# A two-layer kernel on one core: the second layer's output matmuls of a slice issued together instead of in two halves

## The chip, the core and the metric

The kernel runs on one core of a Trainium2 chip. Five engines work side by side, each through its own queue in order: PE (matrix multiply), DVE (vector), ACT (scalar functions), POOL (general) and SP, which here issues the DMAs. The metric is device time in microseconds; less is better. A kernel's time is the median of several runs, and one more execution is taken with the hardware profiler, from which all rows below are read.

## The reference

8192 tokens of width 192 pass through a dynamic convolution of 7 taps (softmax over the taps, 8 heads), then through two layers with an inner width of 2048:

```
x = attn_out.reshape(B * S, D)                       # 8192 x 192
h = x @ w_in                                         # 192 x 2048
P = a[0] + a[1] * h + a[2] * h2 + a[3] * h3
Q = 1.0 + np.abs(b[0]) * np.abs(h) + np.abs(b[1]) * h2
x = (P / (Q + 1e-06)) @ w_out                        # first layer
h = x @ w_in2
return (h * np.clip(h + 3.0, 0.0, 6.0) / 6.0) @ w_out2   # second layer
```

## The kernel before

The tokens are split into 32 blocks of 256, and a block's inner width into 4 slices of 4 chunks of 128, so there are 128 slices `sl`, numbered through; block `b` has slices 4b to 4b+3. Weights are decoded from 64-bit words at the start and stay on the chip.

**First layer, per slice.** PE multiplies the block's input with the slice's weights (`in1`, two halves of two chunks, ten matmuls each, split into high and low parts in fp32r) into the PSUM tile `h1` (two buffers). ACT makes `u` (absolute value), `w` and `l`; POOL multiplies `w` by `u` (`pool_q`, line 293); ACT takes the logarithm (`act_ln`, 308), the exponential (`act_exp`, 313) and one more step on `w` (`act_q`, 317); DVE does `dve_t`, `dve_t2` and `dve_hi` (322), which writes `ghi`, the high part of the activation. POOL's `pool_m` (330) then multiplies `w` by `ghi` into `m`, DVE's `dve_d` (335) subtracts and sets `h1` free, and POOL's `pool_lo` (343) writes `glo`, the low part. PE's `out1` (361 to 366, two halves of ten matmuls) takes `ghi` and `glo` and sums into `y1` over the block's four slices. After the block's last slice `mid_y`, `mid_head` (ACT), `mid_f` (PE, the fold at line 231), `mid_tail` (ACT) and `lo1h`, `lo1t` (DVE) bring `y1` into the form of an input.

**Second layer, per slice, some five slices later.** PE's `in2` (two halves of ten matmuls, into two PSUM buffers `h2`, which it shares with the transposes and the fold), ACT's `act_r2` (387, per half, writes `r`), DVE's `dve_g2` (393, per half, writes half of `g2`; two buffers), and PE's `out2` (409): for each of four chunks and two groups of 128 tokens a matmul in fp32, which the trace records as two passes, summed into `y2`. After a block's last slice ACT's `evac` copies `y2` out and SP stores it.

**Beside it** the convolution for later blocks: `conv_mul` (162, DVE, in the first blocks also POOL), `conv_sum` (176, DVE), the softmax steps, `x_dup`, `x_hi` and the transpose `xT`.

**What sets the order.** Nothing is written in program order. `op`/`add` record each step with an engine, an estimated cost, a priority (a due time, lines 650 to 700), the steps it comes after and the buffers it takes. `plan()` then simulates all engines with these estimates, always placing the step that can start earliest, ties by priority, and the kernel emits the steps in that order. The queue of every engine is fixed by that list; on the chip each engine waits at the head of its queue for what its next instruction needs. A change to one step's cost, due time or conditions can so move steps on all engines. Numbers of slices below are found in the trace by counting: every step's line appears once per slice (or half).

## Time and profile before

| | |
|---|---|
| runs | 1442.16, 1443.62, 1447.23 us |
| median | 1443.62 us |
| profiled execution, span from first to last instruction | 1440.4 us |
| the median of the runs above that span | 3.2 us |
| PE busy / DVE / ACT / POOL | 1314.3 / 1221.8 / 1044.6 / 1007.2 us |

The profile gives no time of its own for the profiled execution beyond its span. Busy time is the sum of an engine's instructions; a matmul's end is modelled and matmuls overlap, so PE's busy time says where it has work, while the spacing of starts says how long that takes. The first 150 us are loading and decoding of weights, with PE mostly idle; then the pipeline runs until the last block is drained.

### The profile page before, as it was taken

To read this page: it belongs to the slowest core of one execution; us is meant where nothing else is said; L and a number is where in the kernel's file an instruction comes from. 1 tells how busy PE (TensorE), PEld (TensorE's weight loads), DVE (VectorE), ACT (ScalarE), POOL (GpSimd) and SP (SyncE) were. 2 spreads that over 40 slices of the span, in tenths; PEclk is the share of its full clock that TensorE was granted. 3 is DMA by queue.
4 is the path that set the end of the run, shared out by engine and by line. 5 is a ranking of instruction groups with operands and counts; after the bars stand their busy time and mean duration, and the time that the engine had idled before them with its cause. 6 is when DMAs were issued, how large, how long until landed. Compare 5 with 4: busy or idle time off the path is not lost.

```text
span 1440.4 us, 23889 instructions
## 1 busy us (share of the span) xinstructions
PE 1314.3 (91%) x9920; PEld 1297.6 (90%) x9920; DVE 1221.8 (85%) x1197; ACT 1044.6 (73%) x1290; POOL 1007.2 (70%) x433
## 2 busy tenths in 40 slices
PE   1333899999999999999999999999999999999998
PEld 1233899999999999999999999999999999999998
DVE  5999988999988888889888888898888888988662
ACT  2654678787778777777787777777777777777772
POOL 4766677767676777677777776777777777777760
PEclk9666999999999999999999999999999999999999
DMA  7444001000010101001010100001010000000000
GB/s 184 120 137 121 28 7 37 7 27 11 7 37 7 37 7 37 6 1 37 7 38 6 37 6 10 28 6 37 7 37 6 32 12 1 7 7 7 6 7 12
DMA packets 18070, 42.17 MB, mean 29 GB/s; under 512 B 2088, under 2 KB 12328, under 8 KB 17960
## 3 DMA queue, kind: packets, MB, share of 16 engines
q1 hardware_dynamic: 17960, 40.63, 9.2%
q8 instruction: 78, 1.28, 0.4%
q14 instruction: 32, 0.26, 0.1%
HBM read 30.14 MB, written 6.29 MB: 25 GB/s over the span
## 4 chain that ended last, share of the span: by engine, by line
DVE 30%; POOL 23%; PE 19%; ACT 13%; issue 12%; DMA 2%; POOLq 0%; SPq 0%; DVEq 0%; ACTq 0%
POOL m L330 15%; PE h L252 9%; POOL w L293 8%; DVE ghi L322 7%; PE y L409 5%; DVE h L301 4%; DVE g L393 4%; DVE m L335 4%; ACT r L313 3%; DVE l L297 3%; ACT r L387 2%; DVE xc L176 2%; ACT l L286 2%; ACT w L317 2%; ACT u L274 2%
## 5 line engine op out<-in xcount | busy, mean ns | idle before, releaser
L330 POOL TENSOR_TENSOR m<-w,ghi 128x1024 f32<-128x1024 f32 x128 | 350.6, 2739 | 317.7 <-DVE ghi L322 248.1
L252 PE MATMUL h<-xh,wtail 128*128 128x256 f32 x2048 | 417.3, 286 | 1.1 <-DVE xh L212 1.1
L409 PE MATMUL y<-wo,g 128*128 128x192 f32 x2048 | 374.8, 325 | 0.0
L409 PEld LDWEIGHTS y<-wo,g 128*128 128x128 f32 x2048 | 329.5, 190 | 0.1
L293 POOL TENSOR_TENSOR w<-w,u 128x1024 f32<-128x1024 f32 x128 | 307.3, 2400 | 27.5 <-ACT w L279 27.5
L252 PEld LDWEIGHTS h<-xh,wtail 128*128 128x128 f32 x2048 | 323.7, 194 | 1.6 <-DVE xh L212 1.6
L343 POOL TENSOR_TENSOR glo<-m,r 128x1024 fp32r<-128x1024 f32 x128 | 309.8, 2420 | 13.8 <-DVE m L335 10.5
L308 ACT ACTIVATE r<-w,ceps 128x1024 f32<-128x1024 f32 x128 | 147.3, 1151 | 220.4 <-POOL w L293 220.4
L335 DVE SCALAR_TENSOR_TENSOR m<-h,acol,m 128x1024 f32<-128x1024 f32 x128 | 164.0, 1281 | 132.2 <-POOL m L330 132.2
L387 ACT ACTIVATE r<-h,half 128x512 f32<-128x512 f32 x256 | 173.6, 678 | 63.1 <-PE h L252 63.1
L252 PE MATMUL h<-xh,win0hi 128*128 128x256 f32 x512 | 164.7, 322 | 52.7 <-DVE m L335 52.0
L393 DVE SCALAR_TENSOR_TENSOR g<-r,h 128x512 f32<-128x512 f32 x256 | 174.0, 682 | 22.9 <-ACT r L387 22.9
L322 DVE SCALAR_TENSOR_TENSOR ghi<-h,acol,r 128x1024 fp32r<-128x1024 f32 x128 | 163.9, 1280 | 16.3 <-ACT r L313 16.1
L176 DVE TENSOR_REDUCE xc<-prod 128x192 f32<-128x1344 f32 x64 | 166.9, 2607 | 0.0
L297 DVE TENSOR_TENSOR l<-h,l 128x1024 f32<-128x1024 f32 x128 | 155.8, 1217 | 11.6 <-ACT l L286 10.0
L301 DVE SCALAR_TENSOR_TENSOR h<-l,acol,h 128x1024 f32<-128x1024 f32 x128 | 164.2, 1283 | 0.5
L252 PE MATMUL h<-xh,win1hi 128*128 128x256 f32 x512 | 162.0, 316 | 1.6 <-DVE xh L212 0.9
L361 PE MATMUL y<-ghi,wo1h 128*128 128x256 f32 x512 | 157.7, 308 | 2.1 <-DVE xl L205 2.1
L279 ACT ACTIVATE w<-u,bab 128x1024 f32<-128x1024 f32 x128 | 159.2, 1244 | 0.0
L252 PEld LDWEIGHTS h<-xh,win0hi 128*128 128x128 f32 x512 | 100.7, 197 | 60.9 <-issue 32.0
L286 ACT ACTIVATE l<-h,acol 128x1024 f32<-128x1024 f32 x128 | 154.1, 1204 | 1.9 <-DVE h L301 1.9
L252 PE MATMUL h<-xl,win0hi 128*128 128x256 f32 x512 | 147.9, 289 | 0.0
(73 smaller groups left out, 2962.9 us busy)
## 6 DMA issues: line engine op xcount, KB each, us to landing
x<-in_x_dram SPq DMA_DIRECT2D x14, 960.0 KB
st<-in_moe_w_out_dram SPq DMA_DIRECT2D x16, 384.0 KB
out_dram<-osb SPq DMA_DIRECT2D x32, 192.0 KB
st<-in_moe_w_in_dram SPq DMA_DIRECT2D x8, 512.0 KB
wtail<-th SPq DMA_DIRECT2D x16, 256.0 KB
st<-in_moe_w_in_dram SPq DMA_DIRECT2D x8, 256.0 KB
x<-in_x_dram SPq DMA_DIRECT2D x4, 472.5 KB
wg<-in_weight_gen_dram SPq DMA_DIRECT2D x16, 112.0 KB
```

What stands on the lines that cost most here:

```text
L176: nc.vector.tensor_reduce(out=xc[b][:, s, 0:D], in_=prod.pop((b, s)).rearrange("p k h g -> p (h g) k"), axis=AX.X, op=ALU.add,)
L252: nc.tensor.matmul(out=dst, lhsT=l[:, fs], rhs=r, start=(n == 0), stop=(n == len(seq) - 1), skip_group_check=True,)
L293: nc.gpsimd.tensor_tensor(out=e["w"], in0=e["w"], in1=e["u"], op=ALU.mult)
L297: nc.vector.tensor_tensor(out=e["l"], in0=h, in1=e["l"], op=ALU.mult)
L301: nc.vector.scalar_tensor_tensor(out=h, in0=e["l"], scalar=acol[:, 1:2], in1=h, op0=ALU.add, op1=ALU.mult)
L322: nc.vector.scalar_tensor_tensor(out=fl(ghi), in0=h, scalar=acol[:, 0:1], in1=e["r"], op0=ALU.add, op1=ALU.mult)
L330: nc.gpsimd.tensor_tensor(out=m, in0=e["w"], in1=fl(g1[sl][0]).bitcast(F32), op=ALU.mult)
L335: nc.vector.scalar_tensor_tensor(out=e["m"], in0=h, scalar=acol[:, 0:1], in1=e["m"], op0=ALU.add, op1=ALU.subtract)
L343: nc.gpsimd.tensor_tensor(out=fl(glo), in0=e["m"], in1=e["r"], op=ALU.mult)
L387: nc.scalar.activation(out=r, in_=h, func=AF.Relu, scale=1.0 / 6.0, bias=half[:, 0:1])
L393: nc.vector.scalar_tensor_tensor(out=g2[sl][:, hh * 2 : hh * 2 + 2, :].rearrange("p f t -> p (f t)"), in0=r, scalar=1.0, in1=h, op0=ALU.mi ...
L409: nc.tensor.matmul(out=y2[b][:, s, :], lhsT=g[:, f, s * P : (s + 1) * P], rhs=wo2[:, n, :], start=(n == 0 and s == 0), stop=(n == NF - 1), ...
```

## The change

The step `out2` is one per slice instead of one per half. It issues all four chunks (16 passes), is planned with a cost of 2.6 instead of 1.3, has one due time (`t + 7 * T + 6.4`, where the halves had `5.4` and `6.4`), comes after the second half of `dve_g2`, and what waited for the second half (`evac`, the release of `g2`) waits for the whole.

```
-    def out2(sl, half):
+    def out2(sl):
         b, q = divmod(sl, NG)
-        fs = range(half * GF // 2, (half + 1) * GF // 2)
-        if q == 0 and 0 in fs:
+        if q == 0:
             y2[b] = ps_y.tile([P, SUB, D], F32, tag="y2", name="y2")
-        g = g2[sl]
-        for f in fs:
+        g = g2.pop(sl)
+        for f in range(GF):
             n = q * GF + f
             for s in range(SUB):
                 nc.tensor.matmul(
                     out=y2[b][:, s, :], lhsT=g[:, f, s * P : (s + 1) * P], rhs=wo2[:, n, :],
                     start=(n == 0 and s == 0), stop=(n == NF - 1), skip_group_check=True,
                 )
-        if GF - 1 in fs:
-            g2.pop(sl)
...
-        add("evac", "ACT", 0.45, t + 10 * T + 8.2, evac, b, after=[("out2", b * NG + NG - 1, 1)])
+        add("evac", "ACT", 0.45, t + 10 * T + 8.2, evac, b, after=[("out2", b * NG + NG - 1)])
...
-                take=[("g2", 2, [("out2", sl, 1)])] if k == 0 else [])
-            add("out2", "PE", 1.3, t + 7 * T + 5.4 + k, out2, sl, k,
-                after=[("dve_g2", sl, k), done["o2", 2 * q + k]] + prev("out2", k),
-                take=[("y2", 1, [("evac", b)])] if q + k == 0 else [])
+                take=[("g2", 2, [("out2", sl)])] if k == 0 else [])
+        add("out2", "PE", 2.6, t + 7 * T + 6.4, out2, sl,
+            after=[("dve_g2", sl, 1), done["o2", 2 * q], done["o2", 2 * q + 1], ("out2", sl - 1)],
+            take=[("y2", 1, [("evac", b)])] if q == 0 else [])
```

`plan()` gives another order for PE, ACT, DVE and POOL from about slice 4 on; from about slice 32 to slice 121 it repeats every eight slices. Three places in that repeat, at slices 66 to 68:

POOL before, from `pool_lo` of slice 66 on (`w` is `pool_q`, `m` is `pool_m`, `glo` is `pool_lo`; numbers tell buffers apart):

```order
L343 TENSOR_TENSOR glo_7503<-m_7450,r0_7398 128x1024
L330 TENSOR_TENSOR m_7556<-w_7466,ghi_7541 128x1024
L293 TENSOR_TENSOR w_7579<-w_7579,u_7568 128x1024
L343 TENSOR_TENSOR glo_7610<-m_7556,r0_7509 128x1024
L330 TENSOR_TENSOR m_7667<-w_7579,ghi_7653 128x1024
```

POOL now, the same place:

```order
L343 TENSOR_TENSOR glo_7496<-m_7450,r0_7398 128x1024
L330 TENSOR_TENSOR m_7552<-w_7466,ghi_7527 128x1024
L343 TENSOR_TENSOR glo_7592<-m_7552,r0_7498 128x1024
L293 TENSOR_TENSOR w_7581<-w_7581,u_7564 128x1024
L330 TENSOR_TENSOR m_7677<-w_7581,ghi_7662 128x1024
```

`glo` of slice 67 now stands ahead of `w` of slice 68. This is so in one slice of eight; in the other seven the order is the old one.

ACT before, from `act_l` of slice 67 on (`r2` is `act_r2`; `r0` is the logarithm at line 308 and the exponential at 313):

```order
L286 ACTIVATE l_7480<-h1_7402,acol_81 128x1024
L387 ACTIVATE r2_7489<-h2_7452,half_85 128x512
L308 ACTIVATE r0_7509<-w_7466,ceps_84 128x1024
L387 ACTIVATE r2_7514<-h2_7491,half_85 128x512
L313 ACTIVATE r0_7509<-r0_7509 128x1024
L317 ACTIVATE w_7466<-w_7466 128x1024
```

ACT now:

```order
L286 ACTIVATE l_7480<-h1_7401,acol_81 128x1024
L387 ACTIVATE r2_7493<-h2_7452,half_85 128x512
L308 ACTIVATE r0_7498<-w_7466,ceps_84 128x1024
L313 ACTIVATE r0_7498<-r0_7498 128x1024
L317 ACTIVATE w_7466<-w_7466 128x1024
L387 ACTIVATE r2_7539<-h2_7502,half_85 128x512
```

The second `r2` left its place between logarithm and exponential. In slices 67 and 71 it stands behind the exponential's successor, in 68, 69 and 70 ahead of the logarithm, and in 64, 65 and 66 it is where it was.

PE before, from the end of the first half of `in1` of slice 68 on:

```order
L252 MATMUL h1_7516<-xh_7463,win0lo_87 128x256
L252 MATMUL h1_7516<-xh_7463,wtail0_90 128x256 x2
L252 MATMUL h2_7529<-xh_7273,win1hi_88 128x256
L252 MATMUL h2_7529<-xl_7275,win1hi_88 128x256
L252 MATMUL h2_7529<-xh_7273,win1lo_89 128x256
```

PE now:

```order
L252 MATMUL h1_7515<-xh_7463,win0lo_87 128x256
L252 MATMUL h1_7515<-xh_7463,wtail0_90 128x256 x2
L361 MATMUL y1_7324<-ghi_7434,wo1h_92 128x256
L362 MATMUL y1_7324<-ghi_7434,wo1l_93 128x256
L363 MATMUL y1_7324<-ghi_7434,wo1s_94 128x256
L365 MATMUL y1_7324<-glo_7496,wo1h_92 128x256
```

`out1` of slice 66 now follows the first half of `in1` of slice 68; before, the first half of `in2` of slice 62 and the second half of `in1` stood ahead of it.

## Rows read from the trace of the kernel before

**Rows 1.** Busy time by stage: us, then engines' busy us (instructions), PEclk, DMA, GB/s.

```profile
190.00:305.00 115.00, 114.98 (x890) 114.48 (x890) 104.06 (x95) 92.25 (x110) 83.25 (x35) 1.00 0.05 16
...
300.00:1300.00 1000.00, 982.38 (x7513) 971.16 (x7512) 871.72 (x848) 766.99 (x935) 730.49 (x292) 1.00 0.05 18
```

**Rows 2.** The page: span, and the chain that ended last, by engine.

```profile
span 1440.4 us, 23889 instructions
...
DVE 30%; POOL 23%; PE 19%; ACT 13%; issue 12%; DMA 2%; POOLq 0%; SPq 0%; DVEq 0%; ACTq 0%
```

**Rows 3.** Waits from 300 to 1300 us: who waited for whom, total us, times, longest.

```profile
POOL m L330 <- DVE ghi L322: 182.9, 73, 3.4
...
PE yf L231 <- DVE g L393: 10.3, 25, 0.4
...
PE h L252 <- DVE m L335: 6.4, 22, 0.4
```

**Rows 4.** Timeline of PE: start, us, instruction, shapes, count, [idle before <-releaser].

```profile
721.53 0.67 PE L231 MATMUL yf<-ys,fold 128*128 128x256 f32 x2 [0.43 <-DVE g L393]
...
803.98 0.67 PE L231 MATMUL yf<-ys,fold 128*128 128x256 f32 x2 [0.42 <-DVE g L393]
...
806.87 1.47 PE L409 MATMUL y<-wo,g 128*128 128x192 f32 x8
808.04 0.41 PE L361 MATMUL y<-ghi,wo1h 128*128 128x256 f32 x1
808.29 0.28 PE L362 MATMUL y<-ghi,wo1l 128*128 128x256 f32 x1
808.41 0.28 PE L363 MATMUL y<-ghi,wo1s 128*128 128x256 f32 x1
```

**Rows 5.** Chain of waits in the span's last stretch: start, us, what.

```profile
1420.83 1.30 PE y L409 x8
```

**Rows 6.** Chain of waits from 718 to 801 us.

```profile
767.95 2.40 POOL m L330
...
773.79 0.67 ACT r L387
...
776.89 3.53 POOL m L330
```

**Rows 7.** Timeline of POOL at slices 66 to 68.

```profile
782.72 2.41 POOL L343 TENSOR_TENSOR glo<-m,r 128x1024 fp32r<-128x1024 f32 x1
786.96 2.39 POOL L330 TENSOR_TENSOR m<-w,ghi 128x1024 f32<-128x1024 f32 x1 [1.82 <-DVE ghi L322]
790.21 2.39 POOL L293 TENSOR_TENSOR w<-w,u 128x1024 f32<-128x1024 f32 x1 [0.86 <-ACT w L279]
```

**Rows 8.** Timeline of ACT at slice 68.

```profile
788.89 1.24 ACT L279 ACTIVATE w<-u,bab 128x1024 f32<-128x1024 f32 x1
...
792.63 1.15 ACT L308 ACTIVATE r<-w,ceps 128x1024 f32<-128x1024 f32 x1 [2.30 <-POOL w L293]
793.69 0.67 ACT L387 ACTIVATE r<-h,half 128x512 f32<-128x512 f32 x1
794.26 1.04 ACT L313 ACTIVATE r<-r 128x1024 f32<-128x1024 f32 x1
```

**Rows 9.** Timeline of DVE at slices 66 to 68.

```profile
776.64 1.55 DVE L162 TENSOR_TENSOR prod<-x,wk 128x1344 f32<-128x1344 f32 x1
...
789.80 1.28 DVE L335 SCALAR_TENSOR_TENSOR m<-h,acol,m 128x1024 f32<-128x1024 f32 x1
...
793.45 2.93 DVE L162 TENSOR_TENSOR prod<-x,wk 128x1344 f32<-128x1344 f32 x1
796.30 0.68 DVE L393 SCALAR_TENSOR_TENSOR g<-r,h 128x512 f32<-128x512 f32 x1
796.90 1.27 DVE L322 SCALAR_TENSOR_TENSOR ghi<-h,acol,r 128x1024 fp32r<-128x1024 f32 x1
```

**Rows 10.** Timeline of PE: the first half of `in1` of slice 68.

```profile
782.42 0.41 PE L252 MATMUL h<-xh,win0hi 128*128 128x256 f32 x1
```

## The prediction

> **What bounds the kernel now.** The start is no use here: up to about 150 us weights are loaded and decoded, and the first output matmul of the second layer comes after that, so nothing before it can change. I read the stages behind it. From 190 to 305 us TensorE is busy for 114.98 of 115 us; from 300 to 1300 us it is busy for 982.38 of 1000 us, at a granted clock of 1.00 in both [rows 1]. So TensorE is close to being the bound, but in the long stage it is not quite it. The span's own chain says the same: the work that ended last runs for 30% through DVE and 23% through POOL and only 19% through PE [rows 2].
>
> The list of waits for the long stage shows how little of PE's time there has a releaser: 10.3 us where the fold matmul waits for the second layer's activation on DVE, 6.4 us where the first layer's input matmuls wait for DVE, while POOL sits 182.9 us waiting for DVE's `ghi` [rows 3]. The order repeats every eight slices (two blocks of tokens are four slices each). Between two fold matmuls eight slices apart lie 803.98 - 721.53 = 82.45 us [rows 4]. The PE work in it: 480 matmuls at 0.12 us (start to start, 808.29 to 808.41, [rows 4]), 128 passes of the second layer's output at 0.162 (1.30 us for eight, [rows 5]) and about 2 us of transposes and folds (an estimate from the fold's 0.67 us for two, overlapped), 57.6 + 20.7 + 2 = 80.3 us. So PE stands still for 82.45 - 80.3 = 2.1 us in eight slices, and no more than that can be won by taking waits away.
>
> What holds the 82.45 us is a ring through the other engines, seen in the chain of waits inside these eight slices [rows 6]: POOL `m` (2.40 us, 3.53 where DVE's convolution multiply began just ahead of it), POOL `w` of the next slice (2.39, [rows 7]), ACT's logarithm (1.15), an ACT step `r` of the second layer (0.67) that has nothing to do with it but stands between, ACT's exponential (1.04, [rows 8]), DVE `ghi` (1.27, [rows 9]), and POOL `m` again. It has hardly any slack. This is what I cost the change against: not against PE's work, which stays the same, but against the queue positions that shift on ACT, DVE and POOL, because the planner lays out all engines anew.
>
> **The joined matmuls themselves.** Count and size stay: 128 slices of 16 passes. Two things could differ. First, a switch between these fp32 matmuls and the fp32r ones around them might cost a restart, of which the change would save one for nearly every slice. The rows say it doesn't: eight passes start at 806.87, the next kind at 808.04, its second matmul at 808.29. From 806.87 to 808.29 is 1.42 us, and eight times 0.162 plus one 0.12 is 1.416 [rows 4, 5]. The long 0.41 us row right behind is a matmul recorded early, not time lost. A switch costs at most 0.005 us, 0.6 us in all; I take 0. Second, a new wait: all four chunks need both halves of the activation. But in the built order the wait for the second half stands at the first matmul of the second half, not at the head of the eight, so the first 1.30 us run as before. At each of the eight places of the repeat I set the new PE position against the time at which the second activation half ends; the nearest is output 61, whose second half is due at 790 or later (its PE position is the old one), while its activation is the DVE step just ahead of the `m` that (2) below puts at 789.25. Taken at 0; if one place in eight missed by 0.5 us this would be 0.5 per repeat.
>
> **What the new order moves, per eight slices.** (1) On ACT the step `r` stands between logarithm and exponential in every slice of the repeat before; after, in five of eight it doesn't: it is behind the exponential or ahead of the logarithm. Its place costs 794.26 - 793.69 = 0.57 us on the ring [rows 8], so up to 2.85 us could leave the ring.
>
> (2) On POOL, in one slice of eight (67, 75, ...), `glo` now stands ahead of the next slice's `w`. Before, `w` started at 790.21, as soon as ACT's own `w` (788.89 plus 1.24) was there [rows 7, 8]. After, `w` waits for `glo` and that for DVE's `m`. Worked through: the exponential 0.57 earlier puts `m` on POOL at 786.96 - 0.57 = 786.4, to 788.8 (2.39 us). DVE's `m` started at 789.80, behind one activation half that is still ahead of it, so it can come only about as much earlier, 789.25, and ends 1.28 later at 790.5. `glo` (2.41) runs to 792.95, `w` (2.39) to 795.35, the logarithm (1.15) to 796.5, the exponential (1.04) to 797.5. `ghi` of slice 68 stood at 796.90 before [rows 7 to 9]. So `w`, 2.75 us later, makes `ghi` only 0.6 us later: before, `ghi` stood behind a convolution multiply that was held up to 2.93 us (1.55 where nothing holds it) and an activation half, until 796.90 [rows 9].
>
> (3) On PE, output matmuls 66 of the first layer now come two places ahead, right behind the input matmuls of slice 68, at 782.42 + 1.2 = 783.6; their fourth matmul needs `glo` of 66, which POOL ends at 782.72 + 2.41 = 785.13 [rows 7, 10]. A new wait of 785.13 - 784.0 = 1.1 us on PE. Queued behind it are the second half of input 68, second-layer input 62 (which itself moves behind three more runs of ten matmuls, 3.6 us) and all that follows. PE has this 1.1 us to give, since of its 2.1 us some go away: one of the two waits at the fold matmul (0.43 us in its row, [rows 4]) vanishes because the fold moves behind 1.2 us more of matmuls, and one of those at the input matmuls too, since DVE's `m` behind the earlier exponential at 71 comes earlier [rows 3].
>
> (4) The 0.6 us of (2) goes on through `m`, DVE's `m`, the reduction and `ghi` of 69, all tight. At slice 70 the ring wins about 0.25 us back, not 0.57, since the `r` step ahead of the logarithm waits for a PE half that (3) made late. At 71 the exponential is 0.57 earlier, but DVE then takes the activation half behind ACT's next step and the reduction starts late by what is left. Net I get +0.3 us for eight slices, against 82.45. The bounds from the same rows: if (2)'s 0.6 is swallowed and one `r` step is won, -0.57; if (3)'s whole 1.1 us reaches the ring, +1.1.
>
> **Sum.** The repeat holds from about slice 32 to slice 121, 11 repeats: 11 x 0.3 = +3.3 us (bounds -6.3 and +12.1). Ahead of it, in slices 9 to 23, the kernel before has most `r` steps out of the ring already and PE stands still for 0.02 of 115 us [rows 1]. The new order keeps such a stage for up to eight slices more (to 31): -1 us, between -2.1 and 0. The tail: the last eight passes wait for an ACT and a DVE step (0.67 and 0.68, [rows 8, 9]) that 1.30 us of the half ahead of them cover no longer fully: +0.1, between 0 and +0.3. Together +2.4 us. The profiled execution has a span of 1440.4 us [rows 2], and the median of the runs, 1443.62, lies 3.2 us above; I carry that over unchanged: 1442.8 in the profile, **1446 us** as a median of runs, between 1435 and 1456.
>
> **A rule weighed against the trace.** The convolution multiply and POOL's steps stretch each other by turns: POOL's `m` that begins just behind a multiply takes 3.53 us instead of 2.39, and the multiply that begins while POOL works takes 2.93 instead of 1.55 [rows 6, 7, 9]. The Trainium skill, page "SBUF — State Buffer", section "Who interferes with whom", states it as an exclusive lock: a VectorE instruction with two SBUF inputs and a GpSimd instruction that reads SBUF block each other for the whole instruction, and which began first decides who waits. By that rule, the trace agrees so far. What it would do to this change is the second rival.
>
> **Rivals.** A, faster: (1) outweighs (2). For it speaks that the ring loses 0.57 us in five slices of eight and that the stage without these steps ran at PE's pace [rows 1]. Against it: `ghi` of 68 and the reduction behind 71 are held by DVE's queue, not by ACT. If PE becomes the bound all of its 2.1 us goes, 11 x 2.1 + 2.1 = 25 us, 1418; half of that, the likelier, gives about 1431.
>
> B, slower by one mechanism: the order in which POOL's `w` of 68 and the multiply of block 19 begin. By (2) `w` begins at 792.95 and the multiply, at 793.45 before [rows 9], about 0.5 us after it, so the multiply waits and `ghi`, later anyway, doesn't notice. If the multiply comes first, `w` takes 3.53 - 2.39 = 1.14 us more and the logarithm and `ghi` behind it too: 11 x 1.14 = 12.5 us on top, 1459. It decides at 0.5 us, in a place where I trust my times to some 0.3.
> By the Trainium skill's rule just named (page "SBUF — State Buffer") it would come out so as soon as the multiply is first.
>
> C, the change does nothing: the shifts on ACT and POOL cancel within the repeat and the joined matmuls run as in [rows 4], 1443 to 1444.
>
> **How the numbers follow.** My forecast, with its own range 1435 to 1456, gets 0.57; A 0.20, B 0.15, C 0.08. About 0.3% (4.3 us) is what a measurement here can tell from no change, so faster means below 1439.3 and slower above 1447.9. Of the forecast's 0.57 I put 0.08 below, 0.29 within and 0.20 above; A gives 0.19 to faster and 0.01 to same, B all to slower, C all to same. That makes faster 0.27, same 0.38, slower 0.35. The range goes from 1431, half of A, to 1457, short of B; about 0.2 lies outside.
>
> **What would show it.** In the changed kernel: the output row of the second layer in runs of 16 passes with no idle ahead of it; the fold's wait for DVE halved; a new PE wait on POOL's `glo` at line 365, about 1 us once in eight slices; POOL's `glo` ahead of `w` there with a wait for DVE's `m`; 82.5 to 83.2 us between fold matmuls eight slices apart. A distance near 80.4 with PE busy throughout would be A; a stretched `w` of 3.5 us once in eight slices would be B. I am wrong if the long wait of POOL at `w` sets in more often than once in eight slices, or if switching between the two kinds of matmul turns out to cost time after all.

## The result

The changed kernel takes 1462.6 us (median; runs from 1461.0 to 1463.0) against 1443.3 us for the kernel before on the same chip: a ratio of 1.0127, 95% interval 1.0115 to 1.014. It is slower by about 19 us. The forecast was 1446 us with a range of 1431 to 1457; the result lies outside. The profiled execution has a span of 1460.6 us, against 1440.4 [rows 2]. The 3.2 us between span and median that the forecast carried over came to 2.0.

The same step in both traces shows where the 20.2 us arise. The table gives the start of the first matmul of `in1` of a slice, and the end of ACT's last copy `evac`:

| | before | after | difference | since the row above |
|---|---|---|---|---|
| slice 8 | 162.16 | 163.14 | 0.98 | |
| slice 24 | 328.96 | 330.68 | 1.72 | +0.7 |
| slice 26 | 348.82 | 357.17 | 8.35 | **+6.6** |
| slice 32 | 410.65 | 418.87 | 8.22 | -0.1 |
| slice 120 | 1318.18 | 1336.17 | 17.99 | **+9.8** |
| last `evac` ends | 1437.72 | 1457.93 | 20.21 | **+2.2** |

The first 1 us is no loss: different executions of kernels that are alike up to there differ at slice 8 by as much. Three losses remain: one of 6.6 us at a single place, one of 9.8 us spread evenly over eleven repeats (0.9 us per eight slices), and one of 2.2 us at the end.

### The profile page after: what moved, and what is told of

Read it like the earlier page. It is cut to its first block, busy times and chain, and to the rows that moved or that the text cites. A ratio compares the mean times of both kernels' runs of the same rounds, so it can differ in the third digit from the quotient of the medians.

```text
span 1460.6 us, 23913 instructions
## 1 busy us (share of the span) xinstructions
PE 1317.1 (90%) x9920; PEld 1298.9 (89%) x9920; DVE 1230.3 (84%) x1197; ACT 1054.7 (72%) x1290; POOL 1008.3 (69%) x433
## 4 chain that ended last, share of the span: by engine, by line
DVE 39%; POOL 24%; PE 15%; ACT 11%; issue 8%; DMA 2%; POOLq 0%; SPq 0%; DVEq 0%; ACTq 0%
POOL m L330 13%; POOL w L293 8%; DVE ghi L322 8%; PE h L252 7%; DVE xc L176 7%; DVE m L335 6%; PE y L408 4%; DVE h L301 4%; ACT r L313 4%; DVE l L297 4%; DVE g L393 4%; ACT r L308 3%; POOL glo L343 2%; DMA st<-in_moe_w_in_dram 1%; DVE sg L143 1%
## 5 line engine op out<-in xcount | busy, mean ns | idle before, releaser
L408 PE MATMUL y<-wo,g 128*128 128x192 f32 x2048 | 354.2, 326 | 0.2 <-DVE g L393 0.2
L252 PE MATMUL h<-xh,win0hi 128*128 128x256 f32 x512 | 156.9, 306 | 65.8 <-DVE m L335 65.1
L365 PE MATMUL y<-glo,wo1h 128*128 128x256 f32 x512 | 147.6, 288 | 10.4 <-POOL glo L343 10.3
L252 PE MATMUL h<-xh,win1hi 128*128 128x256 f32 x512 | 153.4, 300 | 0.3 <-DVE g L393 0.3
```

What stands on the lines that cost most here:

```text
L252: nc.tensor.matmul(out=dst, lhsT=l[:, fs], rhs=r, start=(n == 0), stop=(n == len(seq) - 1), skip_group_check=True,)
L408: nc.tensor.matmul(out=y2[b][:, s, :], lhsT=g[:, f, s * P : (s + 1) * P], rhs=wo2[:, n, :], start=(n == 0 and s == 0), stop=(n == NF - 1), ...
```

## The profile of the changed kernel

Busy time by stage, columns as in [rows 1]:

```profile
190.00:305.00 115.00, 114.39 (x883) 113.67 (x883) 103.19 (x96) 90.61 (x109) 82.25 (x34) 1.00 0.05 16
300.00:1300.00 1000.00, 970.68 (x7395) 959.05 (x7394) 865.73 (x835) 764.88 (x919) 721.72 (x288) 1.00 0.05 18
```

The page: span and the chain that ended last, as in [rows 2]:

```profile
span 1460.6 us, 23913 instructions
...
DVE 39%; POOL 24%; PE 15%; ACT 11%; issue 8%; DMA 2%; POOLq 0%; SPq 0%; DVEq 0%; ACTq 0%
```

Waits from 300 to 1300 us, as in [rows 3]:

```profile
POOL m L330 <- DVE ghi L322: 226.9, 93, 4.1
...
POOL glo L343 <- DVE m L335: 24.6, 13, 2.8
...
PE h L252 <- DVE m L335: 14.0, 12, 4.4
...
PE y L365 <- POOL glo L343: 9.8, 12, 0.9
...
PE yf L231 <- DVE g L393: 4.7, 11, 0.4
```

TensorE is busy for 970.7 of 1000 us instead of 982.4, and the chain now runs for 39% through DVE instead of 30%. Two waits of TensorE are new or larger: 12 times for `glo`, and for DVE's `m`, the longest 4.4 us. The wait at the fold is half of [rows 3].

Timeline of TensorE: two folds eight slices apart, the new wait for `glo`, and a joined output row.

```profile
608.21 0.67 PE L231 MATMUL yf<-ys,fold 128*128 128x256 f32 x2 [0.42 <-DVE g L393]
...
691.57 0.67 PE L231 MATMUL yf<-ys,fold 128*128 128x256 f32 x2 [0.42 <-DVE g L393]
...
796.87 0.38 PE L365 MATMUL y<-glo,wo1h 128*128 128x256 f32 x1 [0.83 <-POOL glo L343]
...
817.91 2.76 PE L408 MATMUL y<-wo,g 128*128 128x192 f32 x16
```

Between the folds lie 691.57 - 608.21 = 83.36 us; before it was 82.45 [rows 4]. The sixteen passes run in one row with nothing idle ahead or within.

## The experiments

All kernels below have the same instructions as before or after; only the order of the queues differs. A function put between the plan and the emission, `relist`, takes the planned list apart into one queue for each engine, lets `edit` move entries, and merges the queues again. Each diff shows `edit`, or says what it does.

### Which queue carries the loss

**TensorE's order alone, and all others alone.** The first kernel has after's order on TensorE and before's order on ACT, DVE and POOL; the second the reverse (before's halves on TensorE).

```
+ for e in ("ACT", "DVE", "POOL"):              # e1, put into after
+     queue[e] = [by_key[k] for k in ORDER_BEFORE[e]]
+ for e in ("ACT", "DVE", "POOL"):              # e2, put into before
+     queue[e] = [by_key[k] for k in ORDER_AFTER[e]]
```

> PE has the queue of the changed kernel (joined output matmuls), ACT, DVE and POOL have the queues of the kernel before. Theory (the time goes through POOL's glo ahead of w and DVE's softmax ahead of d, not through PE): 1440 to 1450 us, 82.4 to 82.8 us between fold matmuls eight slices apart, no stall of over 3 us at 340 to 350 us. Rival (PE's own order loses it: output 66 comes early and waits 1 us for glo once in eight slices, second-layer inputs come late): 1455 to 1465 us, 83.2 to 83.5 us in eight slices.

> The other way round: PE has the queue of the kernel before (two halves), ACT, DVE and POOL have the queues of the changed kernel. Theory: 1456 to 1465 us, the joined matmuls are not needed for the loss. Rival (PE's own order): 1438 to 1448 us.

Measured 1535.6 us (1.0636, 1.062 to 1.0652) and 1500.2 us (1.0389, 1.0373 to 1.0404). Both are far worse than the whole change, and outside every range that was expected. Waits of TensorE in the first, from 300 to 1300 us:

```profile
PE y L365 <- POOL glo L343: 62.0, 23, 4.7
```

`out1` placed early waits for a `glo` that POOL still makes in the old place. The parts of the new order belong together; taken singly they don't add up to the whole. Where the second kernel loses its time was not traced.

**POOL's swap alone.** One kernel puts `w` ahead of `glo` again in the changed order (14 places), the other makes the swap in the order of before (12 places).

```
+ for sl in [22, *range(27, 116, 8), 119]:      # e3, in after; e4 in before: range(27, 116, 8)
+     swap pool_lo of sl and pool_q of sl + 1 in queue["POOL"]
```

> The changed kernel with one thing undone: at the 14 places where POOL's glo stands ahead of the next slice's w, the two are exchanged; all else as changed. Theory: the 0.93 us that each eight slices lost are back and more, since ACT's shorter way between logarithm and exponential stays (0.44 us in five slices of eight, as far as it lies on the ring): 1440 to 1452 us, 81.5 to 82.5 us in eight slices. Rival (PE's order): 1458 to 1464 us.

> The kernel before with one thing of the change put in: POOL's glo ahead of the next slice's w at 12 places, once in eight slices from slice 27 on. Nothing else. Theory: w starts 2 to 3 us later there, and ghi 0.6 to 1.5 us later, which the ring doesn't win back: 12 x 0.6 to 1.5, so 1450 to 1462 us. Rival (PE's order): 1442 to 1447 us.

Measured 1464.0 us (1.0143, 1.0126 to 1.016), no better than after and at the edge of the rival's range, and 1486.5 us (1.0296, 1.028 to 1.0311), above both ranges. In the first, TensorE's waits for `glo` only grow, from 9.8 to 14.9 us. Two things cancel there: the place between slices 24 and 26 loses 5.1 us instead of 6.6, and eight slices of the repeat lose 1.2 instead of 0.9. So the swap, by itself, is neither the cause nor harmless: with the rest of the new order it makes no difference in the sum, with the old order it costs 3.5 us in every eight slices.

### The joined passes alone

**Joining in before's order**, with the second half moved behind the first (e5), and the first moved to the second (e6):

```
+ for sl in range(NS):
+     halves = [by_key["out2", sl, 0], by_key["out2", sl, 1]]
+     # e5: halves[1] goes right behind halves[0]; e6: halves[0] right ahead of halves[1]
```

> The kernel before with the joining alone: each slice's second half of the output matmuls is put right behind its first half on PE, and no other instruction on any engine changes its place. Theory (joining costs nothing; the planner's new order for the rest does): 1440 to 1448 us, 82.3 to 82.7 us in eight slices, no PE wait at the joined matmuls. Rival (the joined run itself delays what stands behind it by 1.3 us and that reaches the ring): 1450 to 1466 us.

> The same, but the first half is moved down to the second, so that nothing behind it starts later and some inputs of the second layer and second halves of out1 come 1.3 us earlier. Theory: 1440 to 1450 us; a wait of up to 0.8 us once in four slices at the second layer's first input matmuls, which come before their input is ready. Rival: 1450 to 1466 us.

Measured 1450.2 us (1.0053, 1.0038 to 1.0068) and 1447.1 us (1.0032, 1.002 to 1.0044). The first lies at the edge between the two ranges, the second within the theory's. The repeat grows by only 0.06 and 0.07 us per eight slices; most of the rest is lost at one place, 6.0 us between slices 18 and 20 and 2.5 us between 22 and 24. The place in e5, timeline of TensorE:

```profile
268.14 1.47 PE L409 MATMUL y<-wo,g 128*128 128x192 f32 x8
273.17 2.90 PE L409 MATMUL y<-wo,g 128*128 128x192 f32 x8 [3.56 <-DVE g L393]
```

and the same stretch by busy time, columns as in [rows 1]:

```profile
268.00:273.00 5.00, 1.60 (x11) 1.31 (x9) 4.94 (x5) 2.65 (x4) 1.66 (x2) 1.00 0.00 2
273.00:276.00 3.00, 2.83 (x9) 2.84 (x10) 0.11 (x1) 0.00 (x0) 2.03 (x1) 0.54 0.00 0
```

The second eight passes of slice 11 wait 3.56 us for their half of the activation. Then they take 2.90 us instead of 1.47: the granted clock of that stretch is 0.54, after 1.00 in the one ahead. The next kernel, in which this wait is gone, takes 5.2 us less over slices 18 to 20; so much of the 6.0 us is this wait with the slow passes behind it.

**The same without this place**: e5, but slice 11 joined where its second half stood.

```
+     late = sl == 11          # there halves[0] goes ahead of halves[1]
```

> The order of before with both halves of the output matmuls together in the place of the first half, as in e5_join_first, save at slice 11, where they stand together in the place of the second half. In e5_join_first nearly all of the 1.0053 came from slice 11: there the second half of the activation came late, TensorE stood still for 3.56 us and then ran at a granted clock near 0.5 for some 2.5 us. Theory (joining costs nothing where both halves of the activation are there): the 6.0 us at slices 18 to 20 are gone, the repeat keeps its +0.07 us per eight slices, 1443 to 1445 us, ratio 1.000 to 1.002. Rival (joining has a price that turns up at some place anyway, as every joined variant so far lost 2.5 to 6.6 us once): the loss moves to another place, 1447 to 1450 us, ratio 1.003 to 1.005.

Measured 1447.1 us (1.0025, 1.0015 to 1.0035), 2 us above the theory's range and at the lower edge of the rival's. Of the 6.0 us 5.2 are gone, and no single other place took them over; in the profile 1.5 us are lost between slices 12 and 32, 0.8 in the repeat and 1.3 at the end. In the order of before, joining costs 0.07 us per eight slices, and 0.25% (4 us) in all.

### The place that loses 6.6 us

Timeline of DVE, POOL and TensorE in the changed kernel, where the softmax steps (lines 142 to 146) stand ahead of `l` (297) of slice 24 and `m` (335) of slice 23:

```profile
337.35 0.37 DVE L142 TENSOR_REDUCE sg<-wg 128x32 f32<-128x224 f32 x1
337.75 2.26 DVE L143 TENSOR_SCALAR sg<-sg 128x32 f32<-128x32 f32 x1
340.05 0.35 DVE L144 RECIPROCAL sg<-sg 128x32 f32<-128x32 f32 x1
340.44 2.33 DVE L146 TENSOR_TENSOR wk<-wg,sg 128x224 f32<-128x224 f32 x1
342.62 1.20 DVE L297 TENSOR_TENSOR l<-h,l 128x1024 f32<-128x1024 f32 x1
343.74 1.27 DVE L335 SCALAR_TENSOR_TENSOR m<-h,acol,m 128x1024 f32<-128x1024 f32 x1
```

```profile
331.01 2.56 POOL L293 TENSOR_TENSOR w<-w,u 128x1024 f32<-128x1024 f32 x1
337.60 2.38 POOL L330 TENSOR_TENSOR m<-w,ghi 128x1024 f32<-128x1024 f32 x1 [4.02 <-DVE ghi L322]
340.02 2.35 POOL L293 TENSOR_TENSOR w<-w,u 128x1024 f32<-128x1024 f32 x1
```

```profile
345.06 0.58 PE L252 MATMUL h<-xh,win0hi 128*128 128x256 f32 x1 [4.43 <-DVE m L335]
345.44 0.42 PE L252 MATMUL h<-xl,win0hi 128*128 128x256 f32 x1
345.65 0.41 PE L252 MATMUL h<-xh,win0lo 128*128 128x256 f32 x1
```

```profile
345.00:349.50 4.50, 4.44 (x21) 4.44 (x22) 4.50 (x6) 0.59 (x1) 2.37 (x1) 0.50 0.00 0
```

In the kernel before, POOL's `w` and DVE's `m` of slice 23 stood earlier, and the softmax steps came 3.6 us behind that `m`, from 339.07 on:

```profile
325.32 2.54 POOL L293 TENSOR_TENSOR w<-w,u 128x1024 f32<-128x1024 f32 x1
...
335.43 1.28 DVE L335 SCALAR_TENSOR_TENSOR m<-h,acol,m 128x1024 f32<-128x1024 f32 x1
```

Two things come together. `w` of slice 23 begins 5.7 us later than before (that of 22 began 2.4 us later), because `glo` of 22 now stands ahead of it and waits for DVE's `m`: it is the swap of the repeat, here in a slice where the forecast did not count it. And POOL finished its `m` at 339.98, but DVE's `m` begins at 343.74, behind four small steps and `l`; two of the small steps last until POOL's own instruction has ended (339.98 and 342.37). TensorE waits 4.43 us, and then 24 matmuls start 0.213 us apart (345.44 to 345.65) instead of 0.12, 2.2 us more, at a granted clock of 0.50. Together that is the 6.6 us.

**The softmax steps put behind `m`:**

```
+ q = queue["DVE"]; n = place of ("softmax_b", 4)
+ q[n : n + 4] = q[n + 1 : n + 4] + [q[n]]
```

> The changed kernel with one DVE step put back: the second part of the softmax of chunk 4 behind d of slice 23, t and t2 of 24, where it stood before, instead of ahead of them. It touches one place at 337 us only. Theory (there its two small steps wait for POOL, 2.26 and 2.33 us, and d and PE behind them): the PE stall of 4.4 us shrinks to under 2 and 2.5 to 5 us are won, 1457.5 to 1460 us. Rival (the stall comes from POOL's late w of 23 alone): 1462 us.

Measured 1459.8 us (1.0115, 1.0098 to 1.0132): the loss at the place falls from 6.6 to 4.8 us. A shorter wait comes in another step (2.3 us, TensorE for DVE's `g`).

**Three pieces put back**: this, POOL's order at slice 22, and two slices of TensorE and POOL in the repeat, which the next part takes up.

> The changed kernel with three pieces of its order put back at once: TensorE's order in two slices of eight and POOL's w ahead of glo there (as in e7_place_back), POOL's w ahead of glo at slice 22, and the softmax steps of chunk 4 behind d of 23 and t, t2 of 24 (as in e8_softmax_back). Theory (the loss is the sum of these places): repeat +0.37 us per eight slices, 4 us in all; the one-time loss at slices 24 to 26 falls from 6.6 to some 3 us; with the tail 1451 to 1453 us, ratio 1.005 to 1.007. Rival (the one-time loss is the step from one pattern of the order to the other, and an edit only moves the wait): it stays above 4.5 us and the time at 1455 or more.

Measured 1453.5 us (1.007, 1.0055 to 1.0085), just above the theory's range: the repeat has its +0.4 us per eight slices, and the place keeps 4.1 us, between theory and rival. The pieces put back explain about 2.5 of its 6.6 us; e17 below has the same order up to there and loses 2.5 us, as TensorE's clock did not fall in its execution. The trace of this kernel shows one more that was not put back, timeline of DVE:

```profile
333.77 2.61 DVE L176 TENSOR_REDUCE xc<-prod 128x192 f32<-128x1344 f32 x1
336.30 1.27 DVE L322 SCALAR_TENSOR_TENSOR ghi<-h,acol,r 128x1024 fp32r<-128x1024 f32 x1
```

`ghi` of slice 23 stands behind a convolution sum, though its exponential ended at 334.59; in the kernel before it stood ahead of that sum. How much of what is left this makes is not shown.

### The repeat

The pieces of the new order at slices 66 to 68 (and every eighth) are: TensorE's `out1` ahead of `in2`; POOL's `glo` ahead of `w`; and a third that only the trace brought up, DVE's second activation half of slice 61 (`g`, with its ACT step `r`), which moved from ahead of `ghi` of 67 to behind the convolution sum. They were put back in combinations:

```
+ PE (sl % 8 in (4, 5)):  in1:0, in2:0, in1:1, out1:0, out2, out1:1, in2:1      # e7, e14, e15
+ POOL (sl in range(27, 116, 8)):  pool_q of sl + 1 ahead of pool_lo of sl      # e7, e15
+ ACT, DVE (same sl):  act_r2 of sl - 6 ahead of act_exp of sl,
+                      dve_g2 of sl - 6 (second half) ahead of dve_hi of sl     # e15, e18
```

> The changed kernel with two slices of eight (68, 69 and so on) put back on PE into the order that the other slices have: second-layer input ahead of the first layer's output, which then comes 2.4 us later; POOL's glo and w exchanged back with it. Output matmuls stay joined. Theory (what the repeat loses comes from out1 standing ahead of its glo there): the repeat falls from 83.38 to 82.6 us or less, so 1449 to 1454 us, the 6.6 us lost once at 340 us remain. Rival (joining costs in every slice): 1458 to 1464 us.

> The changed kernel with TensorE's order alone put back in two slices of eight (second-layer input ahead of out1, as before); POOL's glo stays ahead of w. Theory (out1 moved ahead, with its wait of 0.99 us for glo, is the larger part of the +0.93): repeat +0.3 to +0.5 us per eight slices, 1455 to 1458 us, as e7_place_back. Rival (POOL's w behind glo costs as much by itself): repeat +0.7 or more, 1460 to 1463 us.

> The changed kernel with one piece put back in one slice of eight: ACT's r and DVE's activation half of 61 (69, ...) ahead of the exponential and ghi of 67, where the change has DVE's half behind the convolution sum. TensorE's and POOL's order stay as changed. Theory (this half behind the convolution sum starts the loss, out1 ahead of the second-layer input only follows): repeat +0.3 us per eight slices or less, below 1456 us. Rival (TensorE's out1 ahead, with its wait for glo, is the cause by itself): repeat unchanged at +0.8 to +1.0, 1460 to 1464 us.

> e7_place_back with one more thing put back: ACT's step r and DVE's activation half of 61 (69, ...) ahead of the exponential and ghi of 67, as before the change. In e7_place_back the joined passes of output 61 waited 0.77 us in the middle for this half. Theory (that wait is the +0.37 us per eight slices that e7 kept): repeat below +0.1 us, 1451 to 1453 us. Rival (the ring pays for r being back, 0.44 us): repeat still +0.3 or more, 1455 to 1458 us.

| put back | us | ratio, 95% interval | per eight slices against before |
|---|---|---|---|
| nothing (after) | 1462.6 | 1.0127, 1.0115 to 1.014 | +0.9 |
| POOL (e3) | 1464.0 | 1.0143, 1.0126 to 1.016 | +1.2 |
| PE (e14) | 1522.9 | 1.0547, 1.0523 to 1.0572 | +6.2 |
| activation half (e18) | 1463.7 | 1.0149, 1.0136 to 1.0162 | +0.9 |
| PE and POOL (e7) | 1456.6 | 1.0094, 1.0079 to 1.011 | +0.4 |
| all three (e15) | 1445.7 | 1.0024, 1.0011 to 1.0037 | -0.5 |

The last column is the distance from slice 32 to slice 120 against before, divided by 11. No single piece put back helps, and all three together remove the loss of the repeat. Against what was expected, e14 lies far outside both of its ranges, e7 between its two, e18 in its rival's, and e15 has the repeat of its theory, with a time below the theory's range. TensorE's order and the activation half without POOL's, and POOL's and the half without TensorE's, were not tried. e14 shows why the pieces hang together. Its waits from 300 to 1300 us, and its busy time in that stage:

```profile
POOL glo L343 <- PE y L366: 47.1, 23, 3.4
```

```profile
300.00:1300.00 1000.00, 942.77 (x6966) 929.71 (x6965) 807.98 (x786) 718.98 (x867) 692.93 (x271) 0.96 0.05 18
```

`glo` has one buffer, which `out1` sets free. With `out1` late again and `glo` still ahead of `w`, POOL stands at `glo`, and `w` and the whole ring behind it. In e7 the third piece shows, timeline of TensorE and DVE:

```profile
796.19 1.47 PE L408 MATMUL y<-wo,g 128*128 128x192 f32 x8
798.27 1.57 PE L408 MATMUL y<-wo,g 128*128 128x192 f32 x8 [0.61 <-DVE g L393]
```

```profile
795.03 2.58 DVE L176 TENSOR_REDUCE xc<-prod 128x192 f32<-128x1344 f32 x1
797.52 0.69 DVE L393 SCALAR_TENSOR_TENSOR g<-r,h 128x512 f32<-128x512 f32 x1
```

The joined passes of output 61 stop in the middle for the half that comes behind the convolution sum. With it ahead of `ghi` again (e15), two folds stand 81.99 us apart:

```profile
727.93 0.59 PE L231 MATMUL yf<-ys,fold 128*128 128x256 f32 x2
...
809.92 0.60 PE L231 MATMUL yf<-ys,fold 128*128 128x256 f32 x2
```

That is less than before's 82.45, with the passes joined. So with the three pieces back the rest of the new order, in which `r` has left the ring in five slices of eight, gains 0.5 us per eight slices: the gain that the forecast's (1) looked for is there, and smaller. What is left of e15's loss is the place at slice 24 (6.8 us) and the end (2.3).

### Is the ring really what holds the repeat?

**The step `r` out of the ring, nothing joined.** e11 moves ACT's `r` behind exponential and `w` in six slices of eight of the kernel before, and DVE's half that needs it behind `ghi`.

```
+ ACT:  act_ln, act_exp, act_q, act_r2          # was act_ln, act_r2, act_exp, act_q
+ DVE:  dve_hi, dve_g2                          # was dve_g2, dve_hi
```

> Before, nothing joined: in slices 30 to 121, in six slices of eight, ACT's step r of the second layer moves from between logarithm and exponential to behind the exponential and the step on w, and DVE's activation half that needs it moves behind ghi. This is the term that the forecast counted as a gain, alone. Theory (the ring of logarithm, exponential, ghi and POOL's m holds the eight slices, and r's place in it costs 0.44 to 0.57 us each): the exponential and ghi come earlier in six slices, the waits of TensorE (2.05 us of the 82.45) go by 1 to 2 us per eight slices, 1423 to 1433 us, ratio 0.986 to 0.993. Rival (DVE's and POOL's places in the queue, not ACT's, hold it): under 0.3 us per eight slices, 1440 to 1445 us. Slower than 1448 if the later activation half makes a second-layer input matmul wait for its PSUM buffer.

Measured 1454.6 us (1.0079, 1.0063 to 1.0095): slower, which neither side had; and not by the one way of getting slower that was named, since TensorE's waits are for DVE's `m` (25.7 us from 300 to 1300, against 6.4 before) and not for a second-layer buffer. The exponentials come 0.44 us earlier behind their logarithms, and `ghi` of 61 comes 0.62 us earlier against its step of before, but two places turn it round: at slice 63 the half stayed ahead of `ghi` and waits for its `r`, and at 64 it stands between `ghi` and the convolution multiply, which then begins behind POOL's `m` and takes 3.46 us instead of 1.55.

**The same at the four clean slices** (61, 64, 65, 68 and so on); at 64 the half goes behind the multiply.

```
+     if sl % 8 not in (0, 1, 4, 5): continue
+     past = 2 if the step behind dve_hi is conv_mul else 1
```

> Before, nothing joined: as e11_r_behind, but only in four slices of eight (61, 64, 65, 68 and so on), with DVE's activation half behind ghi, and at 64 behind the convolution multiply too. Theory (r's place on the ring costs 0.44 to 0.57 us, and e11 lost by two places of DVE): ghi 0.5 to 0.9 us earlier in these slices, TensorE's waits of 2.05 us per eight slices fall by 1 to 1.8, over 11 repeats 1424 to 1433 us. Rival (DVE takes it back as in e11): within 4 us of before, 1439 to 1447.

Measured **1418.0 us (0.983, 0.9817 to 0.9842)**, faster than both kernels and faster than expected. Its chain, its stage and two folds:

```profile
PE 81%; DVE 9%; issue 3%; POOL 2%; ACT 2%; DMA 1%; SPq 1%; DVEq 0%; POOLq 0%; ACTq 0%
```

```profile
300.00:1300.00 1000.00, 997.69 (x7707) 993.59 (x7705) 894.27 (x868) 796.46 (x959) 749.61 (x299) 1.00 0.05 18
```

```profile
712.73 0.60 PE L231 MATMUL yf<-ys,fold 128*128 128x256 f32 x2
...
793.03 0.60 PE L231 MATMUL yf<-ys,fold 128*128 128x256 f32 x2
```

TensorE is busy for 997.7 of 1000 us, the chain lies on it for 81%, and the folds are 80.30 us apart: the floor of 80.3 us that the forecast had added up from the matmuls (2 us of it an estimate, so that the agreement to the second digit is luck). The ACT step and the DVE step were moved together; what each is worth alone was not tried.

**Joined on top of these.** e12 is e11 joined as in e9, e16 is e13 joined as in e6, and e17 is the changed kernel with e15's three pieces, the swap at slice 22 and the softmax steps put back, and `r` out of the ring at two more slices of eight.

> The order of e11_r_behind with the joined output matmuls of e9_join_all_but_one. Theory (joining is free, and r's place is what counts): the time of e11_r_behind within 2 us. Rival (joining costs by itself, or the activation half that e11 makes later is now waited for by all sixteen passes): 3 us or more above e11_r_behind.

> The order of e13_r_behind_four with both halves of the output matmuls together in the place of the second half. There TensorE is the bound: 80.23 us per eight slices, no waits. Theory (joining is free): the period stays at 80.2 to 80.3 us; a loss of 2 to 3 us once in the slices 20 to 24, as in e6_join_second, 1419 to 1422 us. Rival (the later first half holds PSUM or g2 longer and makes second-layer steps wait, or the switches that it saves were worth something): 1424 us or more, or 1416 or less.

> The changed kernel, still joined, with e15_g_in_time's edits, POOL's w ahead of glo at slice 22, the softmax steps of chunk 4 put back as in e8_softmax_back, and ACT's r and DVE's activation half out of the ring at slices 64 and 65 (72, 73 and so on). Theory (the whole loss is order): the repeat falls from e15's -0.52 against before to between -1.5 and -2.2 us per eight slices, the one-time loss from 6.8 to about 4 us; 1424 to 1434 us, faster than before although joined. Rival (the joined passes hold the ring at some other place): not below 1440 us.

Measured 1469.3 us (1.0183, 1.0166 to 1.0199), 1431.8 us (0.9932, 0.9917 to 0.9946) and 1439.0 us (0.9978, 0.9969 to 0.9987). e12 lies 15 us above e11, 1.2 us in each eight slices, as its rival had it; the joined passes themselves wait for their half only 0.2 us in each (2.1 us in 11 waits from 300 to 1300 us), and where the rest arises was not traced. e17 lies between the two expectations, 0.8 us per eight slices better than before instead of 1.5 to 2.2, with 2.5 us lost at slice 24. It is joined and still 3 us faster than before, but `r` at two more slices is no part of the change; that most of the change's loss is order rests on e9, where joining alone costs 4 of the 19 us, and on e15. The theory that joining is free falls with e16: eight slices take 81.24 us instead of 80.30, and the time lies in the rival's range. Set against e13 slice by slice, the 0.96 us arise at two steps, `in2` of 56 (0.28) and `in2` of 60 (0.68), the first second-layer inputs behind a fold. In e16, timeline of TensorE:

```profile
763.52 0.39 PE L252 MATMUL h<-xh,win1hi 128*128 128x256 f32 x1 [0.32 <-DVE g L393]
```

The first half of the output matmuls used to stand ahead of this `in2`; without its 1.30 us `in2` comes that much earlier and waits for its PSUM buffer, which the activation half sets free. e17 pays in the other way, waits from 300 to 1300 us:

```profile
PE y L408 <- DVE g L393: 11.1, 11, 1.0
```

## Why the prediction was wrong, point by point

**The step that failed.** Three terms of the sum were mis-sized. The head, put at -1 us with bounds of -2.1 and 0, measured +7.2 (slices 8 to 32), 6.6 of it at one place; the tail, put at +0.1, measured +2.2; the repeat, put at +3.3 with bounds of -6.3 and +12.1, measured +9.8. The repeat alone would have given 1453, inside the range. What took the result out of it is the head, with the tail: the forecast took the slices in which the new order passes from one pattern into the other for a quiet stage.

**What bounds the kernel: right.** The ring through the logarithm, the exponential, `ghi` and POOL, with TensorE 2.1 us per eight slices short of being the bound. e13 takes one ACT step and one DVE step out of that ring in four slices of eight and reaches the forecast's floor of 80.3 us. Its 1418 us are the figure of rival A, in part by luck: A counted 23 us in the repeats and 2 ahead of them, e13 gains 24 in the repeats and nothing ahead. The kernel had this time in it; the planner's new order did not take it.

**The joined matmuls at 0: nearly right here, with a condition that was named.** Alone in before's order they cost 0.07 us per eight slices and some 4 us in all (e9), most of it outside the repeat; where TensorE is the bound they cost 0.96 us per eight slices (e16). The bound for one missed place in eight, 0.5 us, is what e7 shows (0.61 us of idle time) at just the place that was called nearest, output 61. In the changed kernel this wait doesn't show: there output 61 stands behind ten more matmuls and behind the wait for `glo`, starts at 801.40, and its half is done at 801.18 (800.50 + 0.68 below). The forecast saw this half directly ahead of `m` and took it as given; that it had moved there, behind the convolution sum, was not counted among the edits, and e15 shows that it is one of three that make the loss.

**(1) ACT's step `r`: sized too high.** The forecast took 0.57 us from the distance of two starts. With `r` gone, `ghi` of 67 follows `ghi` of 66 after 796.77 - 787.13 = 9.64 us, against 785.51 - 775.44 = 10.07 before: 0.43 us. e11 and e13 show the same 0.44.

**(2) `ghi` of 68, +0.6 forecast: it measured +0.98.** The chain was the right one. Timelines of the changed kernel, DVE, POOL and ACT:

```profile
796.77 1.28 DVE L322 SCALAR_TENSOR_TENSOR ghi<-h,acol,r 128x1024 fp32r<-128x1024 f32 x1 [0.41 <-ACT r L313]
797.98 2.60 DVE L176 TENSOR_REDUCE xc<-prod 128x192 f32<-128x1344 f32 x1
800.50 0.68 DVE L393 SCALAR_TENSOR_TENSOR g<-r,h 128x512 f32<-128x512 f32 x1
801.09 1.28 DVE L335 SCALAR_TENSOR_TENSOR m<-h,acol,m 128x1024 f32<-128x1024 f32 x1
...
805.20 3.47 DVE L162 TENSOR_TENSOR prod<-x,wk 128x1344 f32<-128x1344 f32 x1
...
809.57 1.28 DVE L322 SCALAR_TENSOR_TENSOR ghi<-h,acol,r 128x1024 fp32r<-128x1024 f32 x1 [0.30 <-ACT r L313]
```

```profile
802.51 2.38 POOL L343 TENSOR_TENSOR glo<-m,r 128x1024 fp32r<-128x1024 f32 x1 [1.88 <-DVE m L335]
804.85 2.40 POOL L293 TENSOR_TENSOR w<-w,u 128x1024 f32<-128x1024 f32 x1
```

```profile
807.29 1.16 ACT L308 ACTIVATE r<-w,ceps 128x1024 f32<-128x1024 f32 x1 [1.20 <-POOL w L293]
808.47 1.06 ACT L313 ACTIVATE r<-r 128x1024 f32<-128x1024 f32 x1
```

From `ghi` of 67 the forecast counted 4.31 us to `m`, 8.0 to `w`, 10.4 to the logarithm, 11.6 to the exponential, 12.6 to `ghi` of 68. Measured: 4.32, 8.08, 10.52, 11.70, 12.80. What is missing are mostly the hand-offs between engines, which the sum of durations left out: 0.24 us over the chain, 0.14 of it from DVE's `m` (ends 802.37) to `glo` (802.51). With the 0.14 of (1) that makes 0.38, the difference between 0.6 and 0.98.

**(3) The new wait for `glo`: right.** 1.1 us forecast; the matmul at 796.87 starts 0.98 us later than its turn, once in eight slices. So is the fold's wait, halved.

**(4) The net, +0.3 us: wrong, and here lies half of the loss.** The forecast let slices 69 to 71 win back part of (2)'s 0.6. They do not: (2) alone has 0.98, and the folds move apart by 0.91. The distance of 83.36 us lies above the 82.5 to 83.2 that were to show the forecast. Its upper bound of +1.1 held: it came to 9.8 us over the repeats instead of 3.3, with 12.1 as the bound. What the net left out is the third piece: e7, with the other two put back, still loses 0.4, and e15, with this one back as well, gains 0.5.

**The head, -1 us: wrong in sign, +7.2 measured.** "The new order keeps such a stage for up to eight slices more" was read from before's quiet stage. The `r` steps did stay out of the ring there. But slices 22 to 26, where the new order passes from one pattern into the other, were not costed step by step; one place there costs 6.6 us, by the swap at slice 22 and the softmax steps ahead of `m`, and in part by moves that no run put back. A range made of a repeat and its bounds held no such place.

**The tail, +0.1 us: 2.2.** The wait that was forecast is there, about 0.36 us between the two halves of the last passes, and another at the step from the repeat to the last slices:

```profile
1357.44 0.39 PE L252 MATMUL h<-xh,win0hi 128*128 128x256 f32 x1 [1.53 <-DVE m L335]
```

**The rivals.** B's time, 1459, is near, but its mechanism is not what happened: `w` of 68 begins first and takes 2.40 us, and it is the multiply that waits (3.47 us). That POOL's `glo` waits for DVE's `m` only once in eight slices (13 times in the stage from 300 to 1300 us) holds as forecast. None of the rivals named the place at slice 24 or the three pieces that hang together.

**What stays open.** Why the planner chooses this order is not tried: whether the longer cost, the later due time or the lost freedom of the first half decides it. Of the 6.6 us at slices 24 to 26, 2.5 to 4.1 were never put back. The 0.7 us of drift between slices 8 and 24 and the 1.5 us that e9 loses between slices 12 and 32 are not traced to a step, nor is the 1.53 us wait at slice 122.

## What to carry to other kernels

When a planner lays out all engines anew, cost the places where its pattern changes as carefully as the repeat: a wait of 4.4 us that occurs once weighed two thirds of what 11 repeats lost. A step that was moved on one queue has partners on others through single buffers; putting back one of them can be far worse than putting back none (1523 us against 1463 in e14), so test them together. And where the chain says that a ring with small slack holds a kernel whose main engine is nearly full, look for a step on that ring that does not belong to it: moving one ACT step and one DVE step in four of eight slices was worth 25 us. Where the steps go matters: the same move in six of eight slices, two of them at places where it set up a new wait, lost 11.5 us (e11).

## What the runs showed of the hardware

TensorE's granted clock fell to half, the lower of its two levels, after a single wait in the middle of a busy stage: after 4.43 us of idle time 24 matmuls ran at 0.50, and in e5 after 3.56 us the stretch of the next output passes at 0.54. The two waits cost 6.6 and 5.2 us, about one and a half times their length. The same wait doesn't always cost the same. e18 has the order of the changed kernel up to there and the same wait of 4.4 us, but the 4.5 us from its end on ran at 0.68, not 0.50, and the place cost 5.7 us. e10 and e17 have the same order up to 378 us and the same wait, 1.76 and 1.75 us; behind it the clock was 0.67 over 5 us in e10 and 1.00 in e17, and the place cost 4.1 and 2.5 us. And where another engine sets the pace, the clock cost nothing: in e12, with TensorE busy for 967.8 of 1000 us, it fell after a wait of 1.75 us in four of ten repeats, and those took 84.6 to 84.7 us like the others.

A DVE step on 32 elements a partition took 2.26 us beside a multiplication on POOL and ended 0.03 us behind it. In the trace of before the same step took 0.18 us the one time that it ran beside no POOL instruction, and in the 12 executions of it from 339 us on it ended 0.03 to 0.04 us behind POOL's; so POOL's instruction held it. The reduction and the reciprocal beside it, 0.37 and 0.35 us, were not held. The Trainium skill, page "SBUF — State Buffer", section "Who interferes with whom", says so: steps of the scalar kind can enter a mode that needs the port pair shared with GpSimd, those with two SBUF inputs need it for the second, and a reduction does not; whoever comes second is blocked until the first is done. The rows agree.

ACT's exponential, which needs the logarithm just ahead of it, starts 0.02 us after that ends (808.47 behind 807.29 + 1.16 = 808.45), while in the kernel before an independent step starts 0.09 us ahead of the logarithm's end (793.69 behind 792.63 + 1.15 = 793.78, [rows 8]). Taking a step from between two dependent ones so saves 0.43 us, not its 0.57.
